# From the fourth quad on, TensorE in 64-row tiles: projections in two phases of half rows, token tiles and small products taking turns in two banks

## Chip, cores, metric

One core of a Trainium2 chip. The runs of different rounds were made on different chips, each with the kernel before beside it (medians of 561.6 to 562.9 us). The metric is device time in microseconds, the median of the executions given. All executions told here are in the fast state but one of e12, which is left out. Ratios are computed as the mean time of one kernel's fast runs over that of the other's of the same rounds, so they are not quite the ratios of the medians that I quote.

## The reference, cut to what matters

```python
# q, k, v: (8 batches, 8 heads, 576, 64)
scores = scale * q @ k^T
scores = where(scores >= max(scores) - tau, scores, -1e9)
attn   = exp(scores - max); attn = attn / (sum(attn) + 1e-9)
x      = (attn @ v).transpose(0, 2, 1, 3).reshape(4608, 512)
h      = x @ w_in                    # 512 -> 2048
g      = h * clip(h + 3, 0, 6) / 6
out    = g @ w_out                   # 2048 -> 512
```

## The kernel before

Attention and the two projections are interleaved. An *item* h is a piece of the first projection (256 columns for 256 or 320 tokens), a *token tile* o the second projection of 128 tokens. A *quad* is four heads of one batch; it is worked in nine *slots* (eight of 128 query rows for two heads, the ninth for the remaining rows). The schedule is manual: every engine runs its instructions in the order in which the program emits them. What one slot emits, cut, as are all diffs below:

```python
for n, sl in enumerate(queue):                 # 16 quads x 9 slots
    sm_exp(prev, 0); sm_exp(prev, 1)           # ScalarE, slot n-1
    sm_max(sl)                                 # VectorE: two maxima, POOL: bias
    h = mm1(item)                              # TensorE: projection h, 8 products 128x128, K=512
    r = mm1_relu(h, on_act=...); mm1_gate(...) # ScalarE or VectorE, VectorE
    sm_recip(prev)                             # VectorE
    mm2_part(bb, mt, part)                     # TensorE: a quarter of a token tile o, 4 products
    ...                                        # output copy on VectorE after the last quarter
    sm_mask(sl, 0); sm_mask(sl, 1)             # ScalarE
    ...                                        # a small product: transposes of k, or attn @ v
    queue[n+1].tiles = scores(...)             # TensorE: 64-row products, fp32
    sm_norm(prev)                              # POOL: two normalisations;
                                               # SyncE: transposing DMA of the result
    flush(); start(loads, 1)                   # SyncE: output stores; loads of q and k
```

PSUM, 8 banks: scores 2 x 2, h 2, token tile 1, small products 1. The scores contract over 64 rows and run as two 64-row tiles side by side; h, token tiles and transposes use all 128 rows.

## Time and profile before

| | before |
|---|---|
| device time | 562.9 us (561.4 to 564.2) |
| TensorE busy | 95% |
| ScalarE, VectorE, POOL busy | 84%, 75%, 54% |
| mean granted TensorE clock | 0.989 |
| a quad (mean of the 7th to 15th) | 31.4 us |

Busy is the share of the span in which the engine has an instruction under way; the quad is read from where its first block of scores starts. The lines stand in the prediction below.

### The profile page before, as it was taken

Reading aid. Unit: us, or ns where it says so; the run is one execution under the profiler, and the core shown is the slowest. Engines: PE = TensorE matmul, PEld = TensorE weight load, DVE = VectorE, ACT = ScalarE, POOL = GpSimd, SP = SyncE. Lnnn points to the kernel's source line nnn. Section 1 sums busy time; section 2 is a strip of 40 time slices with the busy share of each in tenths; the row PEclk is TensorE's granted clock in tenths of the full one; section 3 lists DMA queues with packets and bytes.
Section 4 is the critical chain, followed back from the end, with each engine's and each line's share of the span. In section 5 each row is a group of like instructions: output and inputs, shape, how many; then the busy total and the mean of one; then the engine's idle time right before and its main releaser. Section 6 shows DMA issues by size and latency. Waiting matters only on the chain.

```text
span 562.3 us, 11634 instructions
## 1 busy us (share of the span) xinstructions
PE 535.0 (95%) x3856; PEld 309.3 (55%) x3856; DVE 424.4 (75%) x1040; ACT 470.3 (84%) x999; POOL 305.2 (54%) x646
## 2 busy tenths in 40 slices
PE   7998798899999999999999999999999999999997
PEld 5665455455545565555555565655555565654663
DVE  3588787687878788787878798887978798883440
ACT  4799899798988999989898999899898999983540
POOL 1678878854556555655456555755556555561000
PEclk8899999899999999999999999999999999999999
DMA  5879999997689876978589867987699865453102
GB/s 110 135 110 166 162 160 184 207 148 144 112 159 153 151 153 127 208 139 155 114 150 170 159 137 146 174 160 146 127 137 175 167 124 117 101 109 86 38 20 75
DMA packets 286204, 77.52 MB, mean 138 GB/s; under 512 B 269248, under 2 KB 281536, under 8 KB 286144
## 3 DMA queue, kind: packets, MB, share of 16 engines
q1 hardware_dynamic: 268736, 67.86, 64.8%
q0 software_dynamic: 17408, 8.92, 13.7%
q8 instruction: 30, 0.49, 0.4%
q14 instruction: 30, 0.25, 0.2%
HBM read 36.70 MB, written 9.44 MB: 82 GB/s over the span
## 4 chain that ended last, share of the span: by engine, by line
PE 58%; DVE 11%; ACT 9%; issue 4%; POOL 1%; DMA 1%; SPq 1%; DVEq 0%; POOLq 0%
PE h L353 18%; PE o L382 17%; PE s L256 16%; DVE s L277 5%; ACT s L285 4%; PE av L323 3%; ACT s L290 3%; DVE g L370 2%; DVE r L364 2%; ACT r L362 2%; PE s L262 1%; PE tp L213 1%; PE ar L323 1%; DVE osb L390 1%; POOL pn L298 1%
## 5 line engine op out<-in xcount | busy, mean ns | idle before, releaser
L298 POOL TENSOR_SCALAR pn<-s,rinv 128x576 bf16<-128x576 f32 x288 | 211.6, 745 | 133.5 <-issue 58.5
L277 DVE TENSOR_SCALAR_CACHE_REDUCE s<-s 128x576 f32<-128x576 f32 x288 | 205.9, 752 | 44.9 <-PE s L256 35.2
L285 ACT ACTIVATE s<-s,bias 128x576 f32<-128x576 f32 x288 | 207.1, 766 | 36.8 <-POOL bias L280 35.7
L290 ACT ACTIVATE s<-s 128x576 f32<-128x576 f32 x288 | 192.7, 671 | 0.3
L256 PE MATMUL s<-kT,qT 64*128 64x288 f32 x1024 | 172.7, 435 | 5.4 <-DVE s L277 3.2
L353 PE MATMUL h<-xT,w_in_sb 128*128 128x320 bf16 (+1 forms) x1024 | 145.0, 287 | 5.5 <-DVE g L370 4.6
L382 PE MATMUL o<-w_out_sb,g 128*128 128x512 bf16 x576 | 140.9, 379 | 3.6 <-DVE osb L390 3.0
L353 PEld LDWEIGHTS <-w_in_sb 128*128 128x128 bf16 x1024 | 92.0, 97 | 68.4 <-issue 31.1
L256 PEld LDWEIGHTS s<-kT,qT 64*128 64x128 f32 x1024 | 94.8, 188 | 62.7 <-DVE s L277 24.9
L370 DVE SCALAR_TENSOR_TENSOR g<-r,h 128x512 bf16<-128x512 f32 (+1 forms) x128 | 96.4, 754 | 41.2 <-ACT r L362 39.3
L280 POOL TENSOR_SCALAR bias<-m 128x1 f32<-128x1 f32 x288 | 54.4, 189 | 69.0 <-DVE s L277 48.2
L382 PEld LDWEIGHTS <-g 128*128 128x128 bf16 x576 | 55.6, 98 | 58.2 <-issue 9.8
L362 ACT ACTIVATE r<-h,three 128x640 f32<-128x640 f32 (+1 forms) x74 | 54.4, 737 | 21.1 <-PE h L353 20.4
L290 ACT ACTIVATION_READ_ACCUMULATOR s<-s 128x1 f32 x288 | 54.2, 188 | 0.0
L364 DVE TENSOR_SCALAR r<-h 128x512 f32<-128x512 f32 (+1 forms) x54 | 40.5, 751 | 0.0
L390 DVE TENSOR_SCALAR osb<-o 128x512 f32<-128x512 f32 x31 | 21.0, 676 | 22.2 <-PE o L382 22.2
L323 PE MATMUL av<-pT,vm 128*64 128x512 bf16 x256 | 34.6, 392 | 2.0 <-ACT kT L203 2.0
L323 PEld LDWEIGHTS <-vm 128*64 128x64 bf16 x512 | 18.1, 111 | 25.2 <-issue 18.3
L293 DVE RECIPROCAL rinv<-rsum 128x2 f32<-128x2 f32 x144 | 23.0, 160 | 10.2 <-ACT s L290 9.5
L335 DVE CAST xT<-av 128x512 bf16<-128x512 f32 x32 | 21.8, 681 | 5.6 <-PE av L326 5.3
L277 DVE DVE_READ_ACCUMULATOR s<-s 128x1 f32 x288 | 23.9, 83 | 0.0
L388 ACT ACTIVATE osb<-o 128x512 f32<-128x512 f32 x5 | 3.0, 597 | 23.9 <-PE o L382 23.9
(42 smaller groups left out, 255.9 us busy)
## 6 DMA issues: line engine op xcount, KB each, us to landing
km<-in_k_dram SPq DMA_DIRECT2D x64, 128.0 KB, 3.0
out_dram<-osb SPq DMA_DIRECT2D x32, 256.0 KB, 2.4
nq<-in_q_dram SPq DMA_DIRECT2D x96, 72.0 KB, 2.7
vm<-in_v_dram POOLq DMA_DIRECT2D x16, 256.0 KB, 5.4
nq<-in_q_dram SPq DMA_DIRECT2D x16, 128.0 KB, 3.9
w_in_sb<-in_moe_w_in_dram POOLq DMA_DIRECT2D x16, 128.0 KB, 4.1
w_out_sb<-in_moe_w_out_dram POOLq DMA_DIRECT2D x16, 128.0 KB, 4.5
pT<-pn SPq DMA_TRANSPOSE x119, 3.4
```

Source lines behind the costliest of these rows:

```text
L256: nc.tensor.matmul(tiles[a][:, hf, 0:HALF], qT_of(pair)[a * 64:(a + 1) * 64, t * P:(t + 1) * P], keys(pair, a, hf), start=True, stop=True)
L277: nc.vector.tensor_scalar(out=sl.s[:, i, :].rearrange("p (a b) -> p a b", a=2), in0=ps[:, :, 0:HALF], scalar1=1.0, scalar2=None, op0=Alu.m ...
L280: nc.gpsimd.tensor_scalar(out=sl.bias[:, i:i + 1], in0=sl.m[:, i:i + 1], scalar1=-scale, scalar2=tau, op0=Alu.mult, op1=Alu.add)
L285: nc.scalar.activation(out=s, in_=s, func=Act.Prelu, bias=sl.bias[:, i:i + 1], scale=scale, alpha=REJECT)
L290: nc.scalar.activation(out=s, in_=s, func=Act.Exp, accum_out=sl.rsum[:, i:i + 1])
L298: nc.gpsimd.tensor_scalar(out=pn[:, i, :], in0=sl.s[:, i, :], scalar1=sl.rinv[:, i:i + 1], scalar2=1.0, op0=Alu.mult, op1=Alu.mult)
L323: nc.tensor.matmul(ps[a * 64:(a + 1) * 64, :], vm[:, 2 * hp + a, c * D:(c + 1) * D], pT[:, 5 * a + c, cols], start=(c == 0), stop=False)
L353: nc.tensor.matmul(hps[:, n, 0:w], w_in_sb[:, ki, (ni + n) * P:(ni + n + 1) * P], xT[b][:, ki, c0:c0 + w], start=(ki == 0), stop=(ki == KI ...
L362: nc.scalar.activation(out=r, in_=hps, func=Act.Relu, bias=three[:])
L364: nc.vector.tensor_scalar(out=r, in0=hps, scalar1=3.0, scalar2=0.0, op0=Alu.add, op1=Alu.max)
L370: nc.vector.scalar_tensor_tensor(out=gbuf[:, ni:ni + 2, c0:c0 + w], in0=r, scalar=6.0, in1=hps, op0=Alu.min, op1=Alu.mult)
L382: nc.tensor.matmul(o_ps[0], gbuf[:, ni, mt * P:(mt + 1) * P], w_out_sb[:, ni, :], start=(ni == 0), stop=(ni == NI - 1))
```

## The change

The intent: a slot goes back and forth between 128-row and 64-row products, and TensorE loses 93 to 100 ns at each change of form (worked out in the prediction below). So h and the token tiles are made of 64-row products too, except that h keeps its 128-row products in a slot that has neither a token tile nor a small product. Two 64-row tiles run side by side (the score products of a pair start 7 ns apart), so the work should take no longer. But two row tiles may not write one bank at the same time (point 2 of what the prediction takes from the Trainium skill). So an h item has two *phases*: in phase 0 row tile a makes half a of the output in bank a, in phase 1 the tiles change banks. Between phases the second must wait for the first to have been written, and a wait of TensorE on itself is made by a *relay*: a no-operation on SyncE that waits for a later product of TensorE, and for which the first product of the next phase waits. Cut to its core:

```diff
+    class Banks:
+        def products(self, phase, insts):
+            follows(insts[0], self)
+            if self.phase not in (None, phase):
+                relay = nc.sync.nop(nofuse=True)
+                tc.add_manual_dep(relay.ins, self.after.ins.name, SYNC, reason="end of a phase")
+                tc.add_manual_dep(insts[0].ins, relay.ins.name, SYNC, reason="next phase")
+            self.phase, self.after = phase, None
...
+    def mm1_phase(item, hps, phase):
+        for ki in range(KI):
+            for a in range(2):
+                n, c = a ^ phase, row_tile(a)          # row_tile(a) = slice(64 * a, 64 * a + 64)
+                insts.append(nc.tensor.matmul(
+                    hps[:, n, 0:w], w_in_sb[c, ki, (ni + n) * P:(ni + n + 1) * P], xT[b][c, ki, c0:c0 + w], ...))
+        h_banks.products(phase, insts)
...
+            if item:
+                mm1_phase(item, h, 0)
+            if phases:                                  # half a token tile in slots 0, 1, 3, 4
+                mm2_phase(*phases[0][0], phases[0][1], nis)
+            for job in small:                           # slots 2, 5, 7, 8
+                evicts.append(job())
+            if item:
+                mm1_phase(item, h, 1)
+            if phases:
+                mm2_phase(*phases[-1][0], phases[-1][1], range(nis.stop % NI, NI))
...                                                     # slot 6: a whole token tile if more than one is waiting
-        if slot != 8 and todo1:                         # h stood ahead of recip
-            h = mm1(item) ...
         if prev is not None:
             sm_recip(prev)
```

Token tile and small products now share two banks in turn. The order of starts on SyncE (transposing DMA, stores, loads at the end of a slot) is as it was.

More of the change, by code (lines that the diff above doesn't have):

```diff
@@ L43 @@
     N1 = 22
-    N2 = 28
+    N2 = 27
+    DH = d_model // 2
     scale = 1.0 / math.sqrt(D)
@@ L63 @@
     ps_o = ctx.enter_context(tc.psum_pool(name="ps_o", bufs=1))
-    ps_m = ctx.enter_context(tc.psum_pool(name="ps_m", bufs=1))
     ctx.enter_context(tc.manual_schedule())
@@ L189, with bank, row_tile, __init__ @@
     turn = 0
-    def bank(name):
+    obank = ps_o.tile([P, 2, 512], F32, tag="o", name="o")
+    def bank():
         nonlocal turn
         turn += 1
-        if now < N2 and turn % 2:
-            return ps_o.tile([P, 512], F32, tag="o", name=name)
-        return ps_m.tile([P, 512], F32, tag="m", name=name)
+        return obank[:, turn % 2, :]
+    def row_tile(a):
+        return slice(64 * a, 64 * a + 64)
+    SYNC = mybir.DependencyInfo(mybir.DependencyClass.Sync, mybir.DependencyReason.DATA)
+    groups = []
+    class Banks:
+        def __init__(self):
+            self.phase = self.after = None
+            groups.append(self)
+        def products(self, phase, insts):
[5 more added lines that the diff above has]
+            self.phase, self.after = phase, None
+    def follows(inst, banks=None):
+        for one in groups:
+            if one is not banks and one.after is None:
+                one.after = inst
+    h_banks, o_banks = Banks(), Banks()
     def copy_out(out, in_):
@@ L209, in main_pe @@
     def main_pe(src, pair):
-        ps = bank("tp")
+        ps = bank()
         n = pair % 2
@@ L219, in transpose_q @@
             ps = main_pe(nq[:, 0:1024].rearrange("p (t h d) -> p t h d", h=4, t=4), pair)
-            return lambda: nc.vector.tensor_copy(out=qT_of(pair)[:, 0:512], in_=ps[:])
+            return lambda: nc.vector.tensor_copy(out=qT_of(pair)[:, 0:512], in_=ps)
         n = pair % 2
@@ L224, in transpose_k @@
     def transpose_k(pair):
-        ps = main_pe(nat[pair // 2][1], pair)
-        return lambda: copy_out(kT_of(pair)[:, 64:576], ps[:])
+        if now < N2:
+            ps = main_pe(nat[pair // 2][1], pair)
+            return lambda: copy_out(kT_of(pair)[:, 64:576], ps)
+        km, n = nat[pair // 2][1], pair % 2
+        insts = []
+        for t in range(4):
+            for a in range(2):
+                c = row_tile(a)
+                insts.append(nc.tensor.transpose(obank[:, a, t * 64:(t + 1) * 64],
+                                                 km[c, t, 2 * n:2 * n + 2, :], identf[c, c]))
+        o_banks.products(0, insts)
+        return lambda: copy_out(kT_of(pair)[:, 64:576].rearrange("p (t a j) -> p a t j", a=2, j=64),
+                                obank[:, :, 0:256].rearrange("p a (t j) -> p a t j", j=64))
     def transpose_rest(quad):
-        ps = bank("tr")
         nq, _, kr = nat[quad]
-        nc.tensor.transpose(ps[:, 0:P], kr[:], identf[:])
-        if by_pe(2 * quad):
-            nc.tensor.transpose(ps[:, P:2 * P], nq[:, 1024:1152], identf[:])
+        qT, kT = qkT[quad]
+        if now < N2:
+            ps = bank()
+            nc.tensor.transpose(ps[:, 0:P], kr[:], identf[:])
+            if by_pe(2 * quad):
+                nc.tensor.transpose(ps[:, P:2 * P], nq[:, 1024:1152], identf[:])
+            both = ps.rearrange("p (w n t) -> p w n t", n=2, t=64)
+            rest = both[:, 0]
+        else:
+            o_banks.products(0, [nc.tensor.transpose(obank[:, a, 256:320], kr[row_tile(a), :],
+                                                     identf[row_tile(a), row_tile(a)]) for a in range(2)])
+            rest = obank[:, :, 256:320]
         def evict():
-            qT, kT = qkT[quad]
-            both = ps[:].rearrange("p (w n t) -> p w n t", n=2, t=64)
             if by_pe(2 * quad):
                 nc.vector.tensor_copy(out=qT[:, :, 512:S], in_=both[:, 1])
-            copy_out(kT[0:64, :, S:S + 64], both[0:64, 0])
-            copy_out(kT[64:P, :, 0:64], both[64:P, 0])
+            copy_out(kT[0:64, :, S:S + 64], rest[0:64])
+            copy_out(kT[64:P, :, 0:64], rest[64:P])
         return evict
@@ L255, in scores @@
                 for a in range(2):
-                    nc.tensor.matmul(tiles[a][:, hf, 0:HALF], qT_of(pair)[a * 64:(a + 1) * 64, t * P:(t + 1) * P],
-                                     keys(pair, a, hf), start=True, stop=True)
+                    inst = nc.tensor.matmul(tiles[a][:, hf, 0:HALF], qT_of(pair)[a * 64:(a + 1) * 64, t * P:(t + 1) * P],
+                                            keys(pair, a, hf), start=True, stop=True)
+                    follows(inst)
             else:
@@ L261, in scores @@
                         pair = 2 * quad + n
-                        nc.tensor.matmul(tiles[a][n * 64:(n + 1) * 64, hf, 0:HALF],
-                                         qT_of(pair)[a * 64:(a + 1) * 64, 512:S], keys(pair, a, hf),
-                                         start=True, stop=True)
+                        inst = nc.tensor.matmul(tiles[a][n * 64:(n + 1) * 64, hf, 0:HALF],
+                                                qT_of(pair)[a * 64:(a + 1) * 64, 512:S], keys(pair, a, hf),
+                                                start=True, stop=True)
+                        follows(inst)
         return tiles
@@ L322, in av @@
             for a in range(2):
-                nc.tensor.matmul(ps[a * 64:(a + 1) * 64, :], vm[:, 2 * hp + a, c * D:(c + 1) * D],
-                                 pT[:, 5 * a + c, cols], start=(c == 0), stop=False)
+                inst = nc.tensor.matmul(ps[a * 64:(a + 1) * 64, :], vm[:, 2 * hp + a, c * D:(c + 1) * D],
+                                        pT[:, 5 * a + c, cols], start=(c == 0), stop=False)
+                follows(inst)
         for a in range(2):
@@ L331, in av_main @@
             xT[b] = x_pool.tile([P, KI, S], BF16, tag="xT", name="xT")
-        ps = bank("av")
-        av(ps[:], pair, pts[pair], slice(0, 512))
+        ps = bank()
+        av(ps, pair, pts[pair], slice(0, 512))
         o0 = 64 if b % 2 else 0
-        nc.vector.tensor_copy(out=xT[b][:, hp, o0:o0 + 512], in_=ps[:])
+        return lambda: nc.vector.tensor_copy(out=xT[b][:, hp, o0:o0 + 512], in_=ps)
     def av_rest(quad):
         b, g = divmod(quad, 2)
-        ps = bank("ar")
+        ps = bank()
         for n in range(2):
@@ L342, in av_rest @@
         o0 = 0 if b % 2 else 512
-        nc.vector.tensor_copy(out=xT[b][:, 2 * g:2 * g + 2, o0:o0 + 64],
-                              in_=ps[:, 0:P].rearrange("p (a b) -> p a b", a=2))
+        return lambda: nc.vector.tensor_copy(out=xT[b][:, 2 * g:2 * g + 2, o0:o0 + 64],
+                                             in_=ps[:, 0:P].rearrange("p (a b) -> p a b", a=2))
     def mm1(item, pool=None):
@@ L355, in mm1 @@
         return hps[:, :, 0:w]
+    def mm1_phase(item, hps, phase):
+        b, ni, c0, w = item
+        insts = []
+        for ki in range(KI):
+            for a in range(2):
+                n, c = a ^ phase, row_tile(a)
+                insts.append(nc.tensor.matmul(
+                    hps[:, n, 0:w], w_in_sb[c, ki, (ni + n) * P:(ni + n + 1) * P], xT[b][c, ki, c0:c0 + w],
+                    start=(phase == 0 and ki == 0), stop=(phase == 1 and ki == KI - 1)))
+        h_banks.products(phase, insts)
     def mm1_relu(hps, on_act):
@@ L371, in mm1_gate, with mm2_phase, mm2_full, mm2_out @@
                                        op0=Alu.min, op1=Alu.mult)
-    o_ps = {}
-    def mm2_part(bb, mt, part, pool=None):
-        if part == 0:
-            if pool:
-                o_ps[0] = pool.tile([P, 2, 512], F32, tag="s", name="o")[:, 0, :]
-            else:
-                o_ps[0] = ps_o.tile([P, d_model], F32, tag="o", name="o")[:]
-        for ni in range(part * 4, part * 4 + 4):
-            nc.tensor.matmul(o_ps[0], gbuf[:, ni, mt * P:(mt + 1) * P], w_out_sb[:, ni, :],
+    def mm2_phase(bb, mt, phase, nis):
+        insts = []
+        for ni in nis:
+            for a in range(2):
+                j, c = a ^ phase, row_tile(a)
+                insts.append(nc.tensor.matmul(
+                    obank[:, j, 0:DH], gbuf[c, ni, mt * P:(mt + 1) * P], w_out_sb[c, ni, j * DH:(j + 1) * DH],
+                    start=(phase == 0 and ni == 0), stop=(phase == 1 and ni == NI - 1)))
+        o_banks.products(phase, insts)
+    def mm2_full(bb, mt, ps):
+        for ni in range(NI):
+            nc.tensor.matmul(ps, gbuf[:, ni, mt * P:(mt + 1) * P], w_out_sb[:, ni, :],
                              start=(ni == 0), stop=(ni == NI - 1))
-    def mm2_out(bb, mt, on_act):
+    def mm2_out(bb, mt, on_act, ps=None):
         osb = o_pool.tile([P, d_model], F32, tag="osb", name="osb")
+        dst = osb[:]
+        if ps is None:
+            ps, dst = obank[:, :, 0:DH], dst.rearrange("p (j c) -> p j c", j=2)
+            o_banks.phase = None
         if on_act:
-            nc.scalar.activation(out=osb[:], in_=o_ps[0], func=Act.Copy, scale=1.0 / 6.0)
+            nc.scalar.activation(out=dst, in_=ps, func=Act.Copy, scale=1.0 / 6.0)
         else:
-            nc.vector.tensor_scalar_mul(out=osb[:], in0=o_ps[0], scalar1=1.0 / 6.0)
+            nc.vector.tensor_scalar_mul(out=dst, in0=ps, scalar1=1.0 / 6.0)
         b0 = 2 * bb * S
@@ L412, in moe_of @@
                 items.append(((b, ni, c0, w), ()))
-            items[-1] = (items[-1][0], [(b // 2, mt, part) for mt in mts for part in range(4)])
+            items[-1] = (items[-1][0], [(b // 2, mt) for mt in mts])
         return items
@@ L431 @@
     queue[0].tiles = scores(0, 0)
-    prev = None
+    prev = mine = None
     for n, sl in enumerate(queue):
@@ L451 @@
         sm_max(sl)
-        if slot != 8 and todo1:
-            item, then = todo1.pop(0)
-            h = mm1(item)
-            r = mm1_relu(h, on_act=(slot in (0, 1, 3, 5)))
-            mm1_gate(item, h, r)
-            todo2.extend(then)
         copies = pe_transpose(queue[n - 2]) if n > 1 and queue[n - 2].on_chip else None
@@ L463 @@
             copies()
-        outs = []
-        pieces = 0 if slot == 3 else 1
-        if slot == 0:
-            second = True
-        if second and slot < 2 and len(todo2) > 1 and todo2[0][1] == todo2[1][1]:
-            pieces, second = 2, False
-        for _ in range(pieces):
-            if todo2:
-                bb, mt, part = todo2.pop(0)
-                mm2_part(bb, mt, part)
-                if part == 3:
-                    outs += mm2_out(bb, mt, on_act=False)
+        late_slot = n >= N2
@@ new lines @@
+        nxt = 2 * quad + 2
+        more = quad + 1 < NQUAD
+        vector, small = [], []
+        if slot == (6 if late_slot else 5) and more:
+            alloc_qk(quad + 1)
+            vector.append(lambda: transpose_q(nxt))
+        if late_slot:
+            if slot == 0:
+                vector.append(lambda: transpose_q(2 * quad + 1))
+            elif slot == 2:
+                small.append(lambda: transpose_k(2 * quad + 1))
+            elif slot == 5:
+                small.append(lambda: av_main(2 * quad - 1))
+                small.append(lambda: av_rest(quad - 1))
+            elif slot == 7 and more:
+                small.append(lambda: transpose_k(nxt))
+                small.append(lambda: transpose_rest(quad + 1))
+        else:
+            if slot == (1 if quad else 2):
+                vector.append(lambda: transpose_q(2 * quad + 1))
+            elif slot == (2 if quad else 3):
+                small.append(lambda: transpose_k(2 * quad + 1))
+            elif slot == 3 and quad > 0:
+                small.append(lambda: av_main(2 * quad - 1))
+            elif slot == 4 and quad > 0:
+                small.append(lambda: av_rest(quad - 1))
+            elif slot == 6:
+                small.append(lambda: transpose_k(nxt))
+            elif slot == 7:
+                small.append(lambda: transpose_rest(quad + 1))
@@ new lines @@
+        if slot == 8:
+            small.append(lambda: av_main(2 * quad))
+        item = None
+        if slot != 8 and todo1:
+            item, then = todo1.pop(0)
+        phases = []
+        if late_slot and slot in (0, 3) and todo2:
+            mine = todo2.pop(0)
+            phases = [(mine, 0)]
+        elif late_slot and slot in (1, 4) and mine:
+            phases, mine = [(mine, 1)], None
+        elif late_slot and slot == 6 and item and len(todo2) > 1:
+            one = todo2.pop(0)
+            phases = [(one, 0), (one, 1)]
@@ new lines @@
+        evicts = []
+        if late_slot and (phases or small):
+            if item:
+                h = ps_h.tile([P, 2, 512], F32, tag="h", name="h")
+                mm1_phase(item, h, 0)
+            if phases:
+                nis = range(16 if len(phases) == 2 else 4)
+                mm2_phase(*phases[0][0], phases[0][1], nis)
[3 more added lines that the diff above has]
+                mm1_phase(item, h, 1)
+                h = h[:, :, 0:item[3]]
+            if phases:
+                mm2_phase(*phases[-1][0], phases[-1][1], range(nis.stop % NI, NI))
+        elif item:
+            h = mm1(item)
@@ L478 @@
+        if item:
+            r = mm1_relu(h, on_act=(slot in ((0, 1, 4, 5) if late_slot else (0, 1, 3, 5))))
+            mm1_gate(item, h, r)
+            todo2.extend(then)
+        outs = []
+        for one, phase in phases:
+            if phase == 1:
+                outs += mm2_out(*one, on_act=False)
         for i in range(2):
             sm_mask(sl, i)
-        evict = None
-        nxt = 2 * quad + 2
-        if slot == (1 if quad else 2):
-            evict = transpose_q(2 * quad + 1)
-        elif slot == (2 if quad else 3):
-            evict = transpose_k(2 * quad + 1)
-        elif slot == 3 and quad > 0:
-            av_main(2 * quad - 1)
-        elif slot == 4 and quad > 0:
-            av_rest(quad - 1)
-            if quad % 2 == 0:
-                todo1.extend(moe_of(quad // 2 - 1))
-        elif slot in (5, 6, 7) and quad + 1 < NQUAD:
-            if slot == 5:
-                alloc_qk(quad + 1)
-                evict = transpose_q(nxt)
-            elif slot == 6:
-                evict = transpose_k(nxt)
-            else:
-                evict = transpose_rest(quad + 1)
-        elif slot == 8:
-            av_main(2 * quad)
@@ L502 @@
-        if evict:
+        for job in vector:
+            evict = job()
+            if evict:
+                evict()
+        if not late_slot:
+            evicts = [job() for job in small]
+        for evict in evicts:
             evict()
+        if slot == (5 if late_slot else 4) and quad > 0 and quad % 2 == 0:
+            todo1.extend(moe_of(quad // 2 - 1))
         if n + 1 < len(queue):
@@ L535, in rest2 @@
         while todo2:
-            bb, mt, part = todo2.pop(0)
-            mm2_part(bb, mt, part, pool=ps_s if count[1] % 3 else None)
-            if part == 3:
-                flush()
-                late.extend(mm2_out(bb, mt, on_act=(count[1] % 2 == 0)))
-                count[1] += 1
+            one = todo2.pop(0)
+            c = count[1] % 4
+            ps = ps_s.tile([P, 2, 512], F32, tag="s", name="o")[:, 0, :] if c % 2 else obank[:, c // 2, :]
+            mm2_full(*one, ps)
+            flush()
+            late.extend(mm2_out(*one, on_act=(count[1] % 2 == 0), ps=ps))
+            count[1] += 1
     for item in todo1:
         rest1(*item)
-    av_main(2 * last + 1)
+    av_main(2 * last + 1)()
     rest2()
-    av_rest(last)
+    av_rest(last)()
     for item in moe_of(B - 1):
```

## The prediction

> **What bounds the kernel now.** I read the page first (shares, chain), then TensorE's timeline in one stretch, then the timelines of the other engines and of the DMA issuer there, since the change adds waits that pass through that issuer.
>
> ```profile
> span 562.3 us, 11634 instructions
> ...
> PE 535.0 (95%) x3856; PEld 309.3 (55%) x3856; DVE 424.4 (75%) x1040; ACT 470.3 (84%) x999; POOL 305.2 (54%) x646
> ...
> PE 58%; DVE 11%; ACT 9%; issue 4%; POOL 1%; DMA 1%; SPq 1%; DVEq 0%; POOLq 0%
> ```
>
> TensorE (PE) is busy 95% and holds 58% of the chain that ended last, so it is the bound. Its timeline over two slots (start, length, group; groups overlap, so I take start to start):
>
> ```profile
> 307.11 1.24 PE L256 MATMUL s<-kT,qT 64*128 64x288 f32 x8
> 308.38 1.03 PE L353 MATMUL h<-xT,w_in_sb 128*128 128x256 bf16 x8
> 309.25 1.03 PE L382 MATMUL o<-w_out_sb,g 128*128 128x512 bf16 x4
> 310.11 0.60 PE L213 MATMUL tp<-identf,km 128*128 128x128 f32 x4
> 310.64 1.24 PE L256 MATMUL s<-kT,qT 64*128 64x288 f32 x8
> 311.81 1.05 PE L353 MATMUL h<-xT,w_in_sb 128*128 128x256 bf16 x8
> ```
>
> A slot is scores, projection h, a quarter of a token tile o, a small product. Single records give the pitch: h 109 ns (136 at 320 columns), o 216, a transpose 109, a pair of score products 242 (the pair starts 7 ns apart, so the two 64-row tiles run together). Four score pairs should take 0.97 us, and the second scores block above takes 311.81 - 310.64 = 1.17. The 0.2 is the price of changing the tile form: the first pair lasts 346 instead of 242 (+104, its weights can't be loaded ahead), and the change to h adds 100. The change into scores adds 93 more (transpose to scores is 202 in place of 109). So entering costs about 197 ns, leaving about 110; o or h to av (128*64) costs 93 + 24.
>
> Now the issuer, on which I think the case turns:
>
> ```profile
> 306.91 1.30 SPq L306 DMA_TRANSPOSE pT<-pn  x1
> 308.30 1.26 SPq L88 DMA_DIRECT2D km<-in_k_dram  x2
> 310.15 1.93 SPq L306 DMA_TRANSPOSE pT<-pn  x1
> 312.13 2.26 SPq L92 DMA_DIRECT2D nq<-in_q_dram  x4
> 314.49 1.31 SPq L306 DMA_TRANSPOSE pT<-pn  x1
> ```
>
> ```profile
> 306.96 0.47 POOL L280 TENSOR_SCALAR bias<-m 128x1 f32<-128x1 f32 x2
> 308.66 1.47 POOL L298 TENSOR_SCALAR pn<-s,rinv 128x576 bf16<-128x576 f32 x2 [1.23 <-DVE rinv L293]
> ```
>
> ```profile
> SPq L306 <- POOL bias L280: 208.0, 100, 6.2
> SPq L306 <- POOL pn L298: 48.2, 28, 6.2
> ```
>
> SyncE's DMA starts go in program order. The transposing DMA of a slot starts when POOL's normalisation ends (308.66 + 1.47 = 310.13, DMA at 310.15), holds SyncE for 1.3 to 1.9 us, and the loads after it for 0.5 to 0.6 us each. Waiting for POOL takes 256 us of the span. Today nothing on TensorE waits for this directly.
>
> **What the Trainium skill says.**
> 1. "TensorEngine Tiling (Array Packing)", Key Properties: "Changing tiling mode (not just tile) drains the TensorE". The trace agrees: 93 to 100 ns at every change.
> 2. The same page, Gotcha 1: two row tiles must not access the same bank at once and software must synchronise. Hence the two phases and the relays.
> 3. "Perfetto Trace Analysis", DMA Instruction — HWDGE (DVE, Sync): the sequencer itself stands in the semaphore wait, and only when descriptors are generated and its semaphore pushed is it "free for the next instruction". The trace agrees: each SPq item above begins after the one before it has ended, and POOL's wait is taken standing.
> 4. "TensorE: Matmul & The Clock Gate", HAM oscillation — how this bites in real kernels: idle gaps over about 3.4 us bring the half clock. The PEclk row of the profile is at 8 tenths in its first slices, where TensorE idles, so it can occur here.
>
> **The change part by part** (from slot 27, the fourth quad, on; a quad is 9 slots).
>
> *Removed: form changes.* Before, per quad: 9 x 197 + 9 x 110 + 3 x 117 ns = 3.1 us. After: AV stays 128*64 and the last slot's scores 64*64, so slots 5, 7 and 8 still change: about 0.75 us. Gain 2.4 us a quad.
>
> *Work on TensorE.* h: 16 products of 64 rows in place of 8 of 128, two at a time, 8 pairs x 109 = 0.87 us, the same. o: 64 products of 256 columns, 32 pairs x 109 = 3.49 us against 16 x 216 = 3.46. Transposes: the same number of weight loads, about the same. Nothing lost.
>
> *Moved.* recip goes ahead of the gate on VectorE (308.24 would become about 306.9), which brings POOL and its DMA forward by about 1.3 us. Evictions and the tail hardly change; the tail after the last AV is 562.3 - 504.5 = 57.8 us.
>
> *Added: relays.* Each phase change is a wait on a SyncE nop which itself waits for a product. Phase 0 of a new h item follows phase 1 of the last one, so the first product of nearly every slot waits for a nop (all but slot 8, which has no item, and slot 6 when it has no token tile). The schedule is manual, so the nop of slot n+1 stands on SyncE behind slot n's transposing DMA, which is for the probabilities of slot n-1, and behind slot n's loads. In the trace above that place (ahead of the DMA at 314.49) is reached at 314.39, by a slot whose h began on TensorE at 308.38: 6 us late.
>
> The chain, with E(n) the end of scores of slot n, S(n) the first product of slot n: two maxima on VectorE end E + 1.57 (start 0.13 after the scores, 2 x 0.68, read-out 0.08); recip 0.16; to POOL 0.26; two normalisations 1.47; DMA 1.31 at the median; nop and LDWEIGHTS about 0.3 (estimate from the 0.13 us of one semaphore hop and 97 ns of one load). So **S(n+1) >= E(n) + 5.1 us + loads of slot n**, and E(n+1) = S(n) + W(n).
>
> W: half a token tile 1.74, h 0.98 on average, scores 1.13 to the end of the last product, and 0.2 for the second relay (a round trip of about 0.65 over four pairs of 0.44) = 4.05 in slots 0, 1, 3, 4. Slot 2: 2.75; 5: 3.8; 6: 2.4 (6.0 in one quad of four); 7: 3.0; 8: 2.5. Loads hold SyncE for 1.3 us in slots 4, 6 and 7, for 2.1 in slots 5 and 8 (four nq of 0.5), an output for 0.55 in slot 2.
>
> One quad from E8 = 0: S0 = 5.1 + 2.1 = 7.2, E1 = 11.25; S1 = 11.1 (not held), E2 = 15.15; S2 = E1 + 5.1 = 16.35, E3 = 19.1; S3 = E2 + 5.65 = 20.8, E4 = 24.85; S4 = 24.7, E5 = 28.75; S5 = E4 + 5.1 + 1.3 = 31.25, E6 = 35.05; S6 free, E7 = 37.3; S7 = E6 + 6.4 = 41.45, next E8 = 44.45. With the slot 6 tile in one of four: **44.7 us a quad**, against 31.4 now (mean from 192.0 to 474.2, nine quads). TensorE then stands idle about a third of the time.
>
> *Sum.* The fifth quad's scores start at 127.2 (the fourth has few items with phases, so I keep it). Ten quads x 44.7 = 447; quads 15 and 16 without loads 42 + 40 = 82; tail 57.8: 714, and 1 us from span to device time: **715 us**.
>
> **Rivals.**
> *A, TensorE stays the bound and the relays are hidden.* 12 quads x 2.4 = 28 us off: 535. For: 95% busy, changes priced exactly, ScalarE has a floor of about 28 us a quad (9 x 2.66 + 2.5 + 1.5 from start-to-start spacings), which allows 29. The mm2 piece between phases is made to hide a relay. Against: it needs the nops to pass SyncE ahead of DMA starts that precede them in the program.
> *B, the relay costs its round trip only*, 0.2 us x about 7 a quad, with waits for the h bank in slots 2 and 5 (scores, 1.0 us, is all that covers relu and gate of 1.4 to 1.6): about 2 us a quad comes back, 555 to 562, within 2%. Against: the same in-order issuer.
> *C, my case but worse.* Idle stretches of over 3.4 us ahead of slot 0 bring the half clock, some 2 us a quad, and the relu on ScalarE delays exp: 740 to 765.
> *D, my case but milder*: DMA issues at their minimum of 1.24 and loads that fall in free time, 41 us a quad less the clock effects: 635 to 680.
>
> **Range and chances.** The waits of C and D put it between 635 and 765. A and B need SyncE to be out of order, which no line shows; I leave them 12% because the parts look laid out with care by someone who expected a gain.
>
> **What would show it.** Right: TensorE's busy share down to about 70%, its largest waits on SyncE or on "issue" in front of the first h product of a slot, SyncE showing the nop right after a load or transposing DMA, slot 0 worst (over 4 us idle), quads of 43 to 46 us, 512-column o products replaced by 256-column pairs at 109 ns. The 346 ns first score pairs gone in slots 1 to 4. Wrong: quads near 29 us and TensorE over 93% busy (A); gaps of 0.1 to 0.3 us only (B); the pairs of h at more than 109 ns (then the tiles don't run together and the sum of work is what failed).

## The result, and the profile after

758.0 us (754.6 to 762.3, 4 runs) against 562.9: the ratio of the fast runs is 1.347 (95% interval 1.339 to 1.355). That is inside the range of 635 to 765, 43 us above the 715 named. The page of the changed kernel:

```profile
span 757.2 us, 15943 instructions
...
PE 579.8 (77%) x5949; PEld 386.8 (51%) x5952; DVE 429.3 (57%) x1041; ACT 470.1 (62%) x998; POOL 305.2 (40%) x646
...
PEclk8999978898888998989988899989998889999999
...
PE 34%; ACT 16%; DVE 15%; SPq 13%; POOL 6%; issue 5%; POOLq 0%; DVEq 0%
...
L417 PE MATMUL h<-xT,w_in_sb 64*128 64x256 bf16 (+1 forms) x1280 | 125.4, 322 | 142.1 <-SPq L220 132.8
```

VectorE, ScalarE and POOL are busy for about as many microseconds as before (429, 470, 305), in a longer span. TensorE's share of the chain that ended last falls from 58 to 34%, and the DMA issuer's rises from 1 to 13%. The last line gives the cause: before the h products of phases TensorE stood idle for 142 us, 133 of them until L220, the relay. The list of waits (engine and line, who was waited for, us in total, times, longest) says it again, and what the issuer itself waited for:

```profile
PE h L417 <- SPq L220: 132.8, 54, 11.0
```

```profile
SPq L359 <- POOL bias L333: 144.2, 52, 9.1
SPq L359 <- POOL pn L351: 94.5, 56, 4.1
```

A relay takes 17 ns once it runs, so it isn't the relay that is long. The issuer's timeline where the 11th quad starts, and TensorE's beside it:

```profile
426.33 1.30 SPq L88 DMA_DIRECT2D km<-in_k_dram  x2
427.82 1.26 SPq L359 DMA_TRANSPOSE pT<-pn  x1
429.12 2.41 SPq L92 DMA_DIRECT2D nq<-in_q_dram  x4
433.04 1.30 SPq L359 DMA_TRANSPOSE pR<-pn  x1
```

```profile
425.40 1.84 PE L307 MATMUL s<-kT,qT 64*128 64x288 f32 x8
431.64 1.03 PE L417 MATMUL h<-xT,w_in_sb 64*128 64x256 bf16 x8 [4.41 <-SPq L220]
...
436.55 1.13 PE L307 MATMUL s<-kT,qT 64*128 64x288 f32 x8
437.52 0.60 PE L417 MATMUL h<-xT,w_in_sb 64*128 64x256 bf16 x8
```

The four loads of q end at 429.12 + 2.41 = 431.53, the relay behind them runs, and h starts at 431.64, after 4.41 us of idleness. Later in the quad the chain goes through softmax; the chain that ended last, from the scores of slot 1 to the first h product of slot 2 (start, length, what):

```profile
436.71 1.03 PE s L307 x8
...
437.81 1.44 DVE s L330 x4
439.25 0.09 DVE rinv L346
...
439.63 1.48 POOL pn L351 x2
...
441.12 1.25 SPq L359
...
442.42 0.02 SPq L220
...
442.49 0.61 PE h L417 x7
```

The scores end at 437.74. From there: maxima, reciprocal, normalisation, the start of the transposing DMA, relay, h at 442.49. That is 4.75 us; the prediction added up 5.1 for the same steps.

TensorE's clock is lower too: 0.901 on the mean. In three stretches of the same quad (us, then busy us of PE, PEld, DVE, ACT, POOL, then granted clock, DMA share and GB/s): the idle one, the h and token tile work of slot 0 after it, and the same amount of work in slot 1:

```profile
427.50:431.60 4.10, 0.00 (x0) 0.00 (x0) 1.01 (x5) 0.86 (x4) 2.14 (x5) 0.74 0.87 167
431.60:436.50 4.90, 4.86 (x48) 3.42 (x50) 1.35 (x2) 2.07 (x4) 0.00 (x0) 0.52 0.80 90
437.50:440.10 2.60, 2.60 (x50) 2.24 (x48) 1.86 (x6) 1.34 (x4) 0.85 (x3) 1.00 0.01 3
```

The same products take 4.9 us at a clock of 0.52 and 2.6 us at 1.00.

### The profile page after: what moved, and what is told of

It reads as the page before. It is cut to its first block, busy times and chain, and to the rows that moved or that the text cites. A ratio compares the mean times of both kernels' runs of the same rounds, so it can differ in the third digit from the quotient of the medians.

```text
span 757.2 us, 15943 instructions
## 1 busy us (share of the span) xinstructions
PE 579.8 (77%) x5949; PEld 386.8 (51%) x5952; DVE 429.3 (57%) x1041; ACT 470.1 (62%) x998; POOL 305.2 (40%) x646
## 4 chain that ended last, share of the span: by engine, by line
PE 34%; ACT 16%; DVE 15%; SPq 13%; POOL 6%; issue 5%; POOLq 0%; DVEq 0%
PE o L443 11%; PE h L417 10%; DVE s L330 8%; ACT s L338 6%; SPq L359 6%; ACT s L343 6%; SPq L92 5%; POOL pn L351 4%; PE h L407 4%; PE o L450 4%; DVE r L429 3%; PE o L376 2%; PE s L307 2%; DVE g L435 2%; ACT r L427 2%
## 5 line engine op out<-in xcount | busy, mean ns | idle before, releaser
L417 PE MATMUL h<-xT,w_in_sb 64*128 64x256 bf16 (+1 forms) x1280 | 125.4, 322 | 142.1 <-SPq L220 132.8
L417 PEld LDWEIGHTS <-w_in_sb 64*128 64x128 bf16 x1280 | 61.2, 104 | 190.4 <-SPq L220 166.6
L443 PE MATMUL o<-w_out_sb,g 64*128 64x256 bf16 x1792 | 129.4, 295 | 0.5 <-DVE xT L397 0.2
L307 PEld LDWEIGHTS s<-kT,qT 64*128 64x128 f32 x1024 | 105.7, 196 | 41.0 <-DVE s L330 15.2
L443 PEld LDWEIGHTS <-g 64*128 64x128 bf16 x1792 | 100.0, 104 | 20.6 <-issue 1.8
L407 PE MATMUL h<-xT,w_in_sb 128*128 128x320 bf16 (+1 forms) x384 | 53.0, 288 | 11.7 <-DVE g L435 11.6
L407 PEld LDWEIGHTS <-w_in_sb 128*128 128x128 bf16 x384 | 35.4, 98 | 33.1 <-DVE g L435 18.4
L376 PE MATMUL o<-pT,vm 128*64 128x512 bf16 x256 | 42.2, 459 | 7.1 <-ACT kT L237 6.7
L376 PEld LDWEIGHTS <-vm 128*64 128x64 bf16 x512 | 25.1, 133 | 34.5 <-issue 29.5
L450 PE MATMUL o<-w_out_sb,g 128*128 128x512 bf16 x125 | 27.8, 379 | 1.3 <-DVE xT L389 1.1
```

What stands on the lines that cost most here:

```text
L307: inst = nc.tensor.matmul(tiles[a][:, hf, 0:HALF], qT_of(pair)[a * 64:(a + 1) * 64, t * P:(t + 1) * P], keys(pair, a, hf), start=True, sto ...
L376: inst = nc.tensor.matmul(ps[a * 64:(a + 1) * 64, :], vm[:, 2 * hp + a, c * D:(c + 1) * D], pT[:, 5 * a + c, cols], start=(c == 0), stop=F ...
L407: nc.tensor.matmul(hps[:, n, 0:w], w_in_sb[:, ki, (ni + n) * P:(ni + n + 1) * P], xT[b][:, ki, c0:c0 + w], start=(ki == 0), stop=(ki == KI ...
L417: insts.append(nc.tensor.matmul(hps[:, n, 0:w], w_in_sb[c, ki, (ni + n) * P:(ni + n + 1) * P], xT[b][c, ki, c0:c0 + w], start=(phase == 0 ...
L443: insts.append(nc.tensor.matmul(obank[:, j, 0:DH], gbuf[c, ni, mt * P:(mt + 1) * P], w_out_sb[c, ni, j * DH:(j + 1) * DH], start=(phase == ...
```

## The experiments

My theory: the relay stands on SyncE behind the starts of DMAs of earlier slots, and this sets the period. Rivals: the 64-row products are themselves slow; the new order of work costs; the relay's own round trip costs.

**e1, 128-row products, relays kept.** The products of each phase use all rows, one bank after the other; the relays are then not needed, but stay.

```diff
-            for a in range(2):
-                n, c = a ^ phase, row_tile(a)
-                insts.append(nc.tensor.matmul(hps[:, n, 0:w], w_in_sb[c, ki, ...], xT[b][c, ki, c0:c0 + w], ...
+            n = phase
+            insts.append(nc.tensor.matmul(hps[:, n, 0:w], w_in_sb[:, ki, ...], xT[b][:, ki, c0:c0 + w], ...
```

(The same in the token tile, in 256-column halves.)

> The changed kernel with 128-row products in the same places (phase 0 makes the first half of the output, phase 1 the second), relays on SyncE kept though nothing needs them. My theory (the relays stand on SyncE behind the transposing DMA and the loads, and that sets the period): still 740 to 780 us. Rival that the 64-row products are what is slow (pairs that don't run together, half-row weight loads): back to 560 to 600 us.

Measured: 763.2 us (2 runs), ratio to before 1.355. Without one 64-row product in h or the token tiles the loss is all there, and TensorE waits for the relay as before:

```profile
PE h L416 <- SPq L220: 123.7, 49, 8.6
```

So the row tiles are not what is slow.

**e2, the same, without relays.**

```diff
-            if self.phase not in (None, phase):
-                relay = nc.sync.nop(nofuse=True)
-                tc.add_manual_dep(...)
```

> The same 128-row products in the same places, and no relays. My theory: 560 to 590 us, near the kernel before, a little above for the uneven slots. Rival that the new order of the work (half and whole token tiles in some slots, none in others, small products moved) is what costs: over 680 us with no relay in it.

Measured: 596.2 us (4 runs), ratio 1.060. e1 and e2 differ in the relays alone: they cost 167 us. What is left, 33 us above the kernel before, is the new order of work (with token tiles in halves of 256 columns and the transposes of k still in 64-row tiles): this kernel has no relay, and no row tiles in h or the token tiles. It was a little more than I had expected (560 to 590). A quad takes 34.3 us (mean of the 7th to 15th), 3.0 more than before; 1.1 of these are TensorE's own busy time (32.1 us a quad against 31.0).

**e3, loads and stores behind the next slot's relays.** A list holds the starts of a slot until the phases of the next slot have been emitted; the transposing DMA stays where it was.

```diff
+        run_pending()                      # after the phases of the slot
...
-        flush()
-        late.extend(outs)
-        start(loads, 1)
+        for o, i in go: issue(lambda o=o, i=i: nc.sync.dma_start(out=i, in_=o))   # go = late
+        late.extend(outs)
+        if loads: issue(loads.pop(0))      # issue: at once before the 4th quad, else into the list
```

> The changed kernel; a slot's loads and output stores are started only after the next slot's relays, the transposing DMA stays ahead of them. My theory, from the same recurrence without the load terms: a quad of 39 us in place of 44.7 by the recurrence, so about 5.5 us a quad less: 680 to 705 us. Rival that the relay's own round trip is what costs: no change, 750 to 765.

Measured: 695.3 us (2 runs), ratio 1.235. As expected: the loads in front of the relays are worth 63 us, of which some is clock (0.946 in place of 0.901).

**e4, the transposing DMA behind the relays too.**

```diff
-            nc.sync.dma_start_transpose(out=sl.dst, in_=...)
+            issue(lambda: nc.sync.dma_start_transpose(out=sl.dst, in_=...))
```

> The changed kernel; the transposing DMA too is started after the next slot's relays, so that no DMA of the slot stands ahead of them. My theory: most of the loss goes: 540 to 590 us (29.0 us of TensorE work a quad, plus 0.2 us for each second relay and waits of up to 1.3 us where loads reach into the next slot). Rival round trip: over 700 us.

Measured: 642.5 us (4 runs), ratio 1.141. The direction is right, the size is a miss: I had said 540 to 590. The issuer's timeline and TensorE's show what I had left out:

```profile
354.35 1.37 SPq L359 DMA_TRANSPOSE pT<-pn  x1
355.81 1.19 SPq L636 DMA_DIRECT2D out_dram<-osb  x2
357.06 1.30 SPq L88 DMA_DIRECT2D km<-in_k_dram  x2
```

```profile
358.48 0.61 PE L417 MATMUL h<-xT,w_in_sb 64*128 64x256 bf16 x8 [2.28 <-SPq L220]
```

From the last slot of a quad into the first of the next SyncE has work without a break, and the relay at the start of the first h item waits for the end of it. The other part is the order of work, which e2 shows to be 33 us by itself and which I had not known when I wrote the 540. e7 and e8 below test the first part.

**e5, idle stretches filled.** Unused products, so that the clock stays up; relays and DMA order as in the changed kernel.

```diff
+        if late_slot and slot in (4, 8):
+            ps = bank()
+            for _ in range(18 if slot == 8 else 10):
+                nc.tensor.matmul(ps, w_in_sb[:, 0, 0:P], w_in_sb[:, 0, 0:512], start=True, stop=True)
```

> The changed kernel with unused products (128x128x512 bf16, 216 ns each: 18 after the scores of a quad's last slot, 10 after those of its fifth) put where TensorE idles most. If the half clock after idle stretches is what lies between my 715 us and the measured 758, TensorE stays at full clock and the time falls by 25 to 45 us, to 715 to 735. If the chain of waits itself is longer than I reckoned, no gain: 750 to 770.

Measured: 725.7 us (2 runs), ratio 1.291, clock back at 0.986:

```profile
core 0: 720.8 us, clock 0.986
```

Adding useless work to TensorE took 32 us off. So about three quarters of the 43 us between my 715 and the 758 are the half clock: e5 shows it as a sum, not slot by slot. The mean quad, 7th to 15th, goes from 46.8 us to 44.0; my recurrence, which knew no clock, had 44.7.

**e6, no relay at the start of an item.** An h item begins with the phase in which the one before ended; its row tiles then write the banks that they wrote last.

```diff
-                mm1_phase(item, h, 0)
+                turned = h_banks.phase or 0
+                mm1_phase(item, h, turned, True)
...
-                mm1_phase(item, h, 1)
+                mm1_phase(item, h, 1 - turned, False)
```

> The changed kernel; an h item begins with the phase in which the last one ended, so that only the relay in its middle is left, none at its start. DMA order as in the changed kernel. My theory: the relay stays behind the same DMAs, and is only needed 0.9 us later in the slot; the recurrence with 4.4 in place of 5.1 us gives 41.65 us a quad for 44.45: 720 to 735 us. Rival round trip: half the relays gone means half the loss gone, about 660.

Measured: 678.3 us (2 runs), ratio 1.206. Better than either number of my theory, and the result is near what the round-trip rival gave, 660. I don't read it in that rival's favour: e3, e4 and e8 keep relays and lose far less, and the round trip, measured in e8 below, is 0.37 us. My reckoning was probably too simple: I had put the middle of an item 0.9 us after its start everywhere, but in slot 5 the products of attention and in slot 6 a whole half-phase of a token tile (32 products, 1.74 us) stand ahead of it, so the relay is needed some 2 us later there. Slot 5 went from 8.5 us on the mean (7th to 15th quad) to 4.8 in this run, slot 0 from 11.0 to 9.4; slot 6 did not get shorter (6.7, then 6.9). The clock (0.954) gives another part. How the 80 us divide between the later need and the clock I have not measured.

**e7 and e8, both together, and the loads spread.** e7 is e4 and e6 in one; e8 also gives the four q loads of a slot to two slots.

```diff
-            loads.append(lambda n=n: load_q(n))            # four DMAs in one slot
+            for a in ((None,) if b < NB else range(2)):
+                loads.append(lambda n=n, a=a: load_q(n, a))  # two DMAs in each of two slots
```

> Both: no relay at the start of an item, and every DMA of a slot started after the next slot's relay. What e4 still waits for (SyncE is full from the last slot of a quad to the first of the next, and in slots 5 to 7) is needed 0.9 us later, at two or three places a quad: 605 to 625 us.

> e7 with the four q loads of a slot given to two slots, so that no slot has more than two loads (1.3 us) beside its transposing DMA of 1.3 us. 590 to 610 us: near the kernel of e2 (596), whose uneven slots it shares, less some of the 2.4 us a quad for form changes.

Measured: e7 612.0 us (4 runs), ratio 1.090; e8 596.4 us (4 runs), ratio 1.061. Both as expected. With SyncE free where a relay is due, nearly all of the loss from relays is gone: e8, with 64-row tiles and relays, is as fast as e2, with neither. Part of this is an offset: from 200 to 480 us TensorE still waits 5.3 us for relays in e8, and is busy 6.5 us less than in e2. In single records of e8 a relay that finds SyncE free goes like this: first token product of the phase in between at 301.511, relay at 301.821, weight load of the next phase at 301.881, its product at 301.958. The piece of four pairs placed between the phases lasts 0.44 us and hides all of it. In slot 2 of the same quad a q load still held SyncE, to 305.90; the relay ran at 305.953, the next phase of h began 0.69 us after the first transpose, and for 0.28 of that TensorE was idle: the same wait as in the changed kernel, in small.

```profile
301.51 0.61 PE L447 MATMUL o<-w_out_sb,g 64*128 64x256 bf16 x8
301.96 0.71 PE L421 MATMUL h<-xT,w_in_sb 64*128 64x320 bf16 x8
...
306.02 0.72 PE L421 MATMUL h<-xT,w_in_sb 64*128 64x320 bf16 x8 [0.28 <-SPq L224]
```

**e9, e10: even token tiles, with and without row tiles.** In e2 and e8 slot 6 lasts 6.4 to 7.0 us, with a whole token tile in every quad, and slots 3 and 4 are mostly without one.

```diff
-        elif late_slot and slot == 6 and item and len(todo2) > 1:
+        elif late_slot and slot == 6 and item and len(todo2) > 2:
```

> e8, and slot 6 makes a whole token tile only where three are waiting, not two; the second one is then left to slots 3 and 4, which in e8 mostly have no token tile. If the uneven slots are what is left of the loss (slot 6 lasts 6.4 to 7.0 us there, slots 3 and 4 3.0 to 3.2), a quad goes from 34.4 to 31 to 33 us: 555 to 580 us. If not, 590 to 600.

> e2 (128-row products, no relays) with the same even token tiles as e9. Against e9 it shows what the 64-row tiles gain in the same schedule: if TensorE sets the end there, up to 2.4 us a quad, e10 at 575 to 595 and e9 15 to 28 us under it; if the slots are set by other engines, the two within 1% of each other as e2 and e8 were.

Measured: e9 595.8 us, e10 596.8 us (4 runs each), ratios 1.059 and 1.062. The tiles moved (slots 3 and 4 now have one in every quad), and the time did not: the first expectation is a miss. What slot 6 lost (6.6 us in e8, 4.0 in e9), slots 3, 4 and 7 gained (together 9.2, then 12.3). In the second pair the times are within 1% of each other, as said for the case that other engines set the slots. The row tiles free TensorE (busy 254.7 us of the 280 from 200 to 480, against 262.9 in e10), and the time gains 1 us:

```profile
200.00:480.00 280.00, 254.71 (x3332) 181.92 (x3328) 217.87 (x530) 236.26 (x511) 146.59 (x311) 1.00 0.84 141
200.00:480.00 280.00, 262.91 (x2243) 175.10 (x2242) 216.20 (x527) 234.65 (x508) 145.85 (x309) 1.00 0.81 140
```

(e9, then e10; PE is the first of the busy times.) Who waited in the same 280 us of e9, TensorE and ScalarE:

```profile
PE h L421 <- SPq L224: 6.9, 9, 1.6
PE o L380 <- ACT kT L241: 6.3, 8, 0.8
PE h L421 <- DVE g L439: 6.0, 16, 0.8
```

```profile
ACT r L431 <- PE h L421: 32.5, 27, 3.0
```

TensorE's waits are spread over several causes. That TensorE does not set the period in this order of work is therefore not shown: it waits 7.2 us for relays in e9 (6.9 here, and 0.3 before token tiles), which e10 does not have, and that is nearly all of the 8.2 us saved. The row tiles may gain, and the remaining relays take it back. Against this speak e11 and e12 below: there the waits for relays are 1.7 and 3.1 us, and the time is the same. ScalarE waits 32.5 us for h in front of a relu; in the kernel before it was 6.1 in the same window.

**e11, e12: two guesses at the rest.** e11 is e9 with the copies of k in slot 7 on VectorE; e12 is e9 with ScalarE's relus in the slots where h comes early.

```diff
-        if 0 <= now < N1:
+        if 0 <= now < N1 or (now >= N2 and now % 9 == 7):     # e11
...
-            r = mm1_relu(h, on_act=(slot in ((0, 1, 4, 5) if late_slot else ...
+            r = mm1_relu(h, on_act=(slot in ((2, 3, 6, 7) if late_slot else ...   # e12
```

> e9 with the copies of k out of the small bank in slot 7 on VectorE, not on ScalarE, where they stand behind exp and keep the bank from the product of slot 8 (0.8 us in e8). A gain of 0 to 0.8 us a quad: 0 to 10 us under e9, perhaps under the kernel before (563).

> e9 with ScalarE's four relus of a quad in slots 2, 3, 6 and 7 in place of 0, 1, 4 and 5. In the slots with a token tile the second phase of h comes after the first piece of the tile, and ScalarE, which is in order, stands before the relu (46 us in e9) with the masks behind it; VectorE would wait at no cost, since its next maxima need later scores anyway. If this is what is left of the loss, 570 to 588 us; if not, 592 to 600.

Measured: e11 598.6 us (4 runs), e12 597.0 us (3 fast runs; a fourth, 605.9, was slow), ratios 1.066 and 1.058, both within noise of e9. Neither guess brought anything; e12 leaves its own open. In e11 TensorE waits longer for the copies of k than before: 11.4 us of the window on VectorE, against 6.3 on ScalarE in e9. In e12 ScalarE still waits for h, 19.7 us of the window for items with phases and 10.0 for those without, so my edit hardly took the suspected wait away (29.7 us in all, against 32.5); and TensorE waits longer for the copies of k on ScalarE (12.0 us against 6.3). What exactly sets the 34 us of a quad in the new order stays open. No version beats the kernel before.

The account in sums of medians: before 562.9; new order of work +33 (e2, 596.2); relays behind DMA starts +167 (e1, 763.2), of which about 32 by the half clock (measured on the changed kernel, e5); 64-row products -5, hardly clear of the scatter (after, 758.0).

## Why the prediction was right, and where its steps were off

- *What bounds it, and the issuer.* Right in the mechanism; TensorE's busy share fell to 77%, not to about 70%, and a quad took 46.8 us, just outside the 43 to 46 named. Nothing on TensorE waited for SyncE before, and this became the bound: e1 against e2 shows it, and e3, e4, e6 and e8 take the loss away in pieces by moving DMA starts behind the relays or relays to a later place.
- *S(n+1) at E(n) + 5.1 us.* Right within 7%: 4.75 in the piece of the chain shown. Slot 0 as the worst, over 4 us idle: right (4.41).
- *The quad of 44.7 us.* The sum was near (44.0 with the clock kept up, e5), its distribution was partly luck. I took slot 6 for empty in three quads of four; the condition there takes a token tile in every quad, and slots 3 and 4 are then mostly without, and without phases or relays. So I had waits in slots 3 and 7 where there are few (slot 7 lasts 3.3 us on the mean), and a short slot 6 (2.4 us; it lasts 6.7). The two errors nearly cancel. The step from 44.45 to 44.7 doesn't come out of the recurrence either: with W of 6.0 in slot 6 it gives 44.8 in one quad of four, 44.5 on the mean.
- *The second relay, 0.2 us a slot.* Off: 0 where the piece of a token tile lies between, as in the record of e8, where the round trip is 0.37 us to the weight load, not the 0.65 that I estimated.
- *The fourth quad as before (36.7 us).* Off: 48.2. Its slots 2, 5, 6 and 7 already have relays; slot 2 alone lasts 14.6 us. This is the largest part of what the clock leaves of the 43 us. With the clock kept up (e5) the fourth quad still puts the start of the fifth 10.9 us late, the ten quads then take 437.1 us where I had 447, and the rest 145.6 where I had 139.8: the errors partly cancel.
- *The half clock* was rival C, "some 2 us a quad". It was 2.8 us, and I left it out of the named 715. This is the term of the sum that was mis-sized: 0 in the sum, 32 us measured. In the stretch shown above the clock record falls to half at 429.5 us, 2.7 us after TensorE's last product began and 2.1 us before the next one; an idle stretch of 3.4 us, as rival C had it, was not needed there.
- *Work on TensorE.* Right for the products: pairs of h mostly at 108 to 110 ns (256 columns) in the records, and four score pairs from 436.55 to 437.52, 0.97 us in place of 1.17, so the price of entering and leaving is gone there. Transposes are faster than I said: a pair each 60 ns. But the gain of 2.4 us a quad did not come. TensorE is busy 31.0 us a quad before, 32.0 in e10 and 30.8 in e9 (7th to 15th quad): the row tiles save 1.2 us against the same order with 128-row products, and the new order takes 1.1 of it. I had overlooked that h stays in 128 rows, with its changes of form, where a slot has no token tile or small product (slots 3 and 4 of most quads in the changed kernel, slot 6 of most in e9); how much of what is missing that explains was not measured.
- *Nothing lost in the moves.* Wrong, and unnoticed by me: the order of work costs 33 us by itself (e2). It hid inside the larger loss.
- *Rivals A and B* are refuted as ends of this kernel. A needed SyncE out of order. B's round trip is hidden in the record of e8. Even with relays cheap (e8, e9) the 28 us of A don't come; the new order of work eats them, and what bounds it stays open.

## What to carry to other kernels

A wait that is sent through an engine inherits all that stands before it in that engine's program: look at where the no-operation sits in the order, not at how busy the engine is, and put starts that wait for late results behind it. A saving priced exactly on the busiest engine (2.4 us a quad here) can be lost in the order of work that it needs (3.0 us a quad here, e2); test the order alone, with the old operations, before building the new ones on it. And where TensorE began to idle in stretches of some microseconds, its clock was part of the loss (32 us, e5): look at the granted clock before explaining a time by waits alone.

## What the Trainium skill lacked or had wrong

- "TensorEngine Tiling (Array Packing)", Key Properties, says that a change of tiling mode drains TensorE, with no price. Here, in the kernel before: 93 to 100 ns for the change, plus the first weight load that can't go ahead (104 ns for fp32 scores, 24 for bf16 attention products).
- The same page, Gotcha 1, leaves the synchronisation of row tiles on one bank to software and says nothing of its cost. Here a round trip from TensorE over a free SyncE took 0.37 us from the start of a product to the waiting weight load, and 0.44 us of other products hid it; behind DMA starts the same relay cost up to 11.0 us.
- "TensorE: Matmul & The Clock Gate", LDWEIGHTS (loading the stationary operand), gives P / 1.2 ns for P columns, 107 ns for 128, and not how closely loads can follow each other. In e8 the records of fp32 loads of 128 columns into 64-row tiles (transposes of k) last 137 to 143 ns, and start, two at a time, 57 to 61 ns after the pair before.
